# A quarter of the turned keys held in PSUM between the layers, and a norm's factor moved into the softmax, in a two-layer decode kernel

## The chip, the cores and the metric

The kernel runs on one core of a Trainium2 chip, in one launch. The metric is the device time of a whole execution in microseconds (us). Four executions of the kernel before gave a median of 1129.24 us, from 1121.21 to 1132.17.

## The reference, cut to what matters

Eight sequences (rows) decode one token each. Two blocks alternate, each twice: an attention block with a cache, and an MLP.

```python
B, Sq, D = 8, 1, 448
Hq, Hkv, Sk, Dh = 16, 8, 4096, 256          # F = 1792, all bfloat16

def _A_ref(x, k_cache, v_cache, wq, wo):     # x is normed
    q = (x @ wq)...                          # B, Hq, Sq, Dh
    scores = einsum("bhqd,bhkd->bhqk", q, k) * (Dh ** -0.5)
    p = softmax(scores); o = einsum("bhqk,bhkd->bhqd", p, v)
    return o... @ wo

x = A_x
x = x + _A_ref(_layernorm(x), A_k_cache, A_v_cache, A_wq, A_wo)
x = x + _B_ref(_layernorm(x), ...)           # norm, w3, gelu, w4
x = x + _A_ref(_layernorm(x), A_k_cache, A_v_cache, A_wq, A_wo)
x = x + _B_ref(_layernorm(x), ...)
```

Both attention blocks read the same caches. With a single token the shifts in the MLP's first half read only padding, so the kernel computes its second half alone. One row's keys of one KV head are 4096 x 256 bfloat16, 2 MiB (2048 KB in the profile), and its values as much. All keys and values are 256 MiB, and whatever is not kept in SBUF from the first layer is read again in the second.

## The kernel before, in words

**Tiles.** A key or value tile (row b, head h) lies on 128 partitions, 32 positions of 256 numbers on each, and is cut into four *quarters* of 4 KB a partition, 0.52 MB in all. SBUF has 30 slots of a quarter (`QUARTERS`, L14). `load` (L602) records one load for each quarter, the planner joins up to four neighbours into one DMA, and `issue_kv` (L590) writes it; L596 is the DMA itself, always on SyncE's queue (SP).

**A front** (L914) is the first half of one row's head in one layer: keys to softmax weights. Keys must be turned, because the scores contract over Dh. `transpose_piece` (L1091) turns half a quarter on TensorE into one of three PSUM banks `psT` (L1099), and DVE or ACT copies the bank back over the same slot (L1107, L1108). Then `sc` (L939) multiplies the turned quarter with the query into the bank `psS` (16 matmuls, L947), DVE copies the scores out and takes the maximum (L959, L962), GpSimd reduces it over partitions (L964), DVE scales and negates it into `nb` (L966), ACT takes two exponentials with `scale=1/16` and a bias from `nb` (L972), GpSimd sums (L976). **A back** (L982) loads the values, multiplies weights and values (32 matmuls `pv`, L1002), folds four partial rows into one (L1014, L1016, L1024, L1030) and multiplies with `wo` (L1049; for the last head of a row L900 and L903).

**What is kept.** In layer 1 (`layer == 0` in the code) heads 3 to 7 are the kept heads (`KEEP_K = 5`): their turned keys stay in SBUF, so that layer 2 of the same row need not load and turn them. Head 7 also keeps its four value quarters (`KEEP_V = 4`). That is 24 of 30 slots by the end of a row's layer 1; six slots are left as a ring through which everything else passes, until the scores of layer 2 free the kept keys again. Heads 0 to 2 are the free heads.

**The border between the layers.** For each row b: fronts and backs of its kept heads, head 7 last; then `mid` (L1131): the MLP (`mlp` L839), which gives x2, then `sums` (L695) and `moments` (L712) for the second attention's norm, then the second layer's queries (`second_queries`, L1140) for head 7 here and for the other heads a little ahead of their fronts. Beside it run the backs of the next row's free heads (12 quarters of values, whose fronts were done before). Then the fronts and backs of layer 2, head 7 first (`l2_heads` counts down, `MIX` L27), and the next row's kept heads. `sums` gets sum and sum of squares of x2 from TensorE, `moments` makes mean, variance and 1/sqrt from them in ten small DVE instructions and a table `t_q` (mean times column sums of wq times 1/sqrt), and the query is `psM * rsy + t_q` (L1145): it waits for all of them.

**The order** is made before the launch by `Plan.schedule` (L131): it has a cost for every instruction, starts on each engine the ready one of the lowest priority number, and chooses for each load a slot and the wait on the matmul that used this slot last (`next_kv` L177). The programs of the engines are then fixed. SP is in order: a load that waits for its slot holds all later loads. Where TensorE would be idle, `filler` (L1266) puts matmuls that compute nothing into a free `psT` bank (L1268)[...].

Of the kernel before, what the change touches and what calls it, by code (L numbers as in the profile page):

```python
# [6 lines left out]
P = 128  # L7
B = 8
D = 448
# [10 lines left out]
RSQRT_STEPS = ((0.703952253, 1.681914091), (0.5, 1.5000003))  # L20
KEEP_K = 5
KEEP_V = 4
MARGIN4, MARGIN2 = 6, 2
REP = 24
AT = (-4, -3, -2)
# [418 lines left out]
def bass_interleave_layers__gqa_block_cached__mixer_s_mlp__decode_kernel(  # L444
# [58 lines left out]
    mom = sb("mom", [P, 3, B], f32)  # L503
    cs_q = sb("cs_q", [P, 32], f32)
    cs_h = sb("cs_h", [P, 14], f32)
    t_q = sb("t_q", [P, 32], f32)
    t_h = sb("t_h", [P, 28], f32)
    var = sb("var", [P, 2, B], f32)
    rsi = sb("rsi", [P, 2, B], i32)
# [185 lines left out]
    def sums(src, skey, n):  # L695


        def mm(t):
            for r in range(n):
                for kc in range(4):  # L700
                    last = t.matmul(psM[:, SC + r * (n + 2):SC + (r + 1) * (n + 2)],
                                    wide(src[:, kc, r:r + 1]), src[:, kc, 0:n + 2],
                                    start=(kc == 0), stop=(kc == 3))
            return last
        pe(mm, 4 * n, rd=[skey, "one"], wr=["psM"], banks=[M])
# [3 lines left out]
        i = r * (n + 2) + n + 1  # L709
        return mom[:, i // B, i % B:i % B + 1]  # L710

    def moments(second, cs, cskey, t_, tkey, n):  # L712


        k = n * (n + 2)
        mo = mom[:, :, :].rearrange("p c n -> p (c n)")[:, 0:k]
        v0 = var[:, 0, 0:n]
        dv(lambda v: v.tensor_single_scalar(mo, psM[:, SC:SC + k], 1.0 / D, ALU.mult),
           rd=["psM"], wr=["mom"], banks=[M])
# [12 lines left out]
        rsqrt(c, n)  # L732
        w = cs.shape[1]
        for r in range(n):
            dv(lambda v, r=r: v.tensor_scalar(t_[:, r * w:(r + 1) * w], cs[:, :], minus_mean(n, r),
                                              rsy[:, c - 1, r:r + 1], ALU.mult, ALU.mult),
               rd=["mom", "rsy", cskey], wr=[tkey] if r == 0 else [(tkey, r)])

    def norm(src, skey, second, B):

# [98 lines left out]
    def mlp(src, skey, n, dst, dkeys):  # L839
# [6 lines left out]
        if few:  # L846

            sums(src, skey, n)
            moments(True, cs_h, "cs_h", t_h, "t_h", n)
# [61 lines left out]
    KEPT_V = {HKV - 1: range(4 - KEEP_V, 4)}  # L911
    done = {}

    def front(layer, b, h):  # L914
# [3 lines left out]
        fronts[0] += 1  # L918
        par, nr, nm = 0, free_p.pop(0), g % NS
        ps, bk = psS, "S"  # L920
        kept_k, kept_v = state.pop((0, b, h)) if layer else ({}, {})
        keep_k = KEPT_K.get(h, ()) if layer == 0 else ()
        if layer == 0:
            def rhs(c):
# [4 lines left out]
                return q2T[b % 2][:, 4 * h + 2 * c:4 * h + 2 * c + 2]  # L929
            qk = [("q2", b, h)]  # L930
        ks = dict(kept_k)
        fresh = [u for u in range(4) if u not in ks]
        ks.update(load(A_k_cache, b, h, fresh, keep_k))
        for u in range(4):
            if u in fresh:
                for pc in range(2):
                    transpose_piece(ks[u], pc)

            def sc(t, u=u, q=ks[u]):  # L939
                last = None  # L940
                for s in range(8):
                    i = 8 * u + s


                    for c in range(2):
                        a = slot_ap(q, s * 256, 256)
                        last = t.matmul(ps[:, 2 * i:2 * i + 2 * REP], a[:, c:256:2],  # L947
                                        bcast(rhs(c), REP, 1), start=(c == 0), stop=(c == 1))
# [17 lines left out]
        plan.op("dve", lambda v: v.tensor_single_scalar(nb[nm][:, :], gm[nm][:, :], -INV_SQRT_DH,  # L966
                                                        ALU.mult), 0.15, "max",
                rd=[("gm", nm)], wr=[("nb", nm)], prio=hi)

        for jj in range(2):  # L970
            def ex(a, jj=jj):
                return a.activation(pT[nr][:, :, :].rearrange("p i j -> p j i")[:, jj, :],  # L972
                                    sview[:, jj, :], ACT.Exp, bias=nb[nm][:, jj:jj + 1],
                                    scale=INV_SQRT_DH, accum_out=rs[nr][:, jj:jj + 1])
            plan.op("act", ex, 0.5, "exp", rd=[("nb", nm), ("sS", nm)], wr=[("pT", nr, jj), ("rs", nr, jj)], prio=hi)
# [4 lines left out]
        state[layer, b, h] = ({u: ks[u] for u in keep_k}, kept_v, nr)  # L980

    def back(layer, b, h):  # L982

        kept_k, vs, nr = state.pop((layer, b, h))
        free_p.append(nr)
        keep_v = KEPT_V.get(h, ()) if layer == 0 else ()
        g = backs[0]
# [96 lines left out]
               rd=["psM", ak], wr=[ok] + (["x3all" if b < B - 2 else "xf"] if layer else []), banks=[M],  # L1084
               name="acc", prio=hi)
        if layer == 0:
            state[layer, b, h] = (kept_k, {u: vs[u] for u in keep_v})

    tcount = [0]

    def transpose_piece(i, pc):  # L1091
        bank = tcount[0] % NT
        tcount[0] += 1

        def tr(t):
            last = None
            for s in range(4):
                src = slot_ap(i, (4 * pc + s) * 256, 256).bitcast(f32)
                last = t.transpose(psT[bank][:, s * P:(s + 1) * P], src, ident_f[:, :])  # L1099
# [4 lines left out]
        def ev(e):  # L1104
            dst = slot_ap(i, pc * 1024, 1024).bitcast(f32)
            if e is nc.vector:
                return e.tensor_copy(dst, psT[bank][:, :])  # L1107
            return e.copy(dst, psT[bank][:, :])  # L1108
        v = plan.op("ev", ev, {"dve": 0.71, "act": 0.6}, "ev", rd=[("psT", bank)],
                    wr=[("s", i, pc)], banks=[("T", bank)])  # L1110
        a.tbank = v.tbank = bank

    s_out = nc.alloc_semaphore("s_out")

# [25 lines left out]
    def second_queries(b, h, prio):  # L1140

        q, src = q2T[b % 2], x2c[b % 2]
        pe(lambda t: q_mms(t, range(4 * h, 4 * h + 4), lambda kc: src[:, kc, 0:1], psM, SC,
                           1, QW), 16, rd=[("x2", b)] + WQ, wr=["psM"], banks=[M], prio=prio)
        dv(lambda v: v.scalar_tensor_tensor(  # L1145
            q[:, 4 * h:4 * h + 4].rearrange("p (c j) -> p c j", c=2),
            psM[:, SC:SC + 4].rearrange("p (j c) -> p c j", c=2), rsy[:, 0, 0:1],
            t_q[:, 4 * h:4 * h + 4].rearrange("p (c j) -> p c j", c=2), ALU.mult, ALU.add),
           rd=["psM", "rsy", "t_q"], wr=[("q2", b, h)], banks=[M], prio=prio)


    dma_once("x", [(x_row[:, 0:D], A_x[:, 0, :], 7168), (x_row[:, D + P:], A_x[:, 0, 3 * P:D], 1024)],
# [174 lines left out]
```

## Time and profile before

| | us |
|---|---|
| median of four executions | 1129.24 |
| the profiled execution | 1130.02 |
| its span, first to last instruction | 1128.2 |
| TensorE busy, of the span | 967.5 (86%) |
| DVE busy | 552.9 (49%) |
| ACT busy | 280.9 (25%) |
| GpSimd busy | 97.6 (9%) |

The mean granted TensorE clock is 0.933. SP's queue moves 446.80 MB in 54784 packets. A page of the profile has the busy shares (part 1), forty slices of the span (part 2: busy tenths, granted clock, share of the 16 DMA engines, GB/s), the DMA queues (3), the chain that ended last (4), and groups of instructions by line with busy time, mean duration in ns and the idle time before them (5). Windows give the same for chosen stretches.

### The profile page before, as it was taken

The page shows a single profiled execution, that of the slowest core. Times are in us where ns is not written, and L with a number is a line of the kernel's source. Part 1 is how long each engine was busy: PE and PEld are TensorE (multiplying, and loading weights), DVE is VectorE, ACT ScalarE, POOL GpSimd, SP SyncE. Part 2 cuts the span into 40 slices and gives each one's busy share as a digit, 9 for nine tenths or more (in the row PEclk, how much of TensorE's full clock was granted, in tenths as well). Part 3 has the DMA queues.
Part 4 walks back from the last instruction along what each step waited for, and adds up shares of the span by engine and source line. Part 5 has one row for each costly group of instructions (what it writes and reads, how often), then busy time and mean ns, then how long its engine had stood idle before and what let it go on. Part 6 is the DMA issues. An engine that isn't in the chain of part 4 may idle for free.

```text
span 1128.2 us, 42331 instructions
## 1 busy us (share of the span) xinstructions
PE 967.5 (86%) x19458; PEld 775.0 (69%) x19458; DVE 552.9 (49%) x1745; ACT 280.9 (25%) x848; POOL 97.6 (9%) x275
## 2 busy tenths in 40 slices
PE   5888888898889897898889887989878998798897
PEld 4677566775669756686567765778566885686674
DVE  4345435455355544555346553565535654365444
ACT  1133112341124301243023410234112330142030
POOL 0001010010100100010010000110010010110010
PEclk9899999999889979899899988999999998999899
DMA  9999999999999999999999999999999999999993
GB/s 329 409 425 421 384 404 424 424 423 380 413 423 425 419 334 418 424 424 417 360 425 424 423 386 384 423 424 422 383 413 424 423 400 378 424 421 405 358 361 154
DMA packets 54962, 449.50 MB, mean 398 GB/s; under 512 B 5872, under 2 KB 9088, under 8 KB 28032
## 3 DMA queue, kind: packets, MB, share of 16 engines
q1 hardware_dynamic: 54784, 446.80, 97.1%
q8 instruction: 152, 2.49, 0.9%
q14 instruction: 26, 0.21, 0.0%
HBM read 446.77 MB, written 0.01 MB: 396 GB/s over the span
## 4 chain that ended last, share of the span: by engine, by line
PE 53%; DMA 36%; issue 5%; DVE 4%; SPq 1%; POOL 0%; ACT 0%
DMA kv<-in_A_k_cache_dram 21%; PE psT L1099 21%; PE psS L947 14%; DMA kv<-in_A_v_cache_dram 14%; PE psP L1002 7%; PE psR L1049 3%; PE psT L1268 2%; PE psM L797 2%; DMA w3x_sb<-in_B_w_dram 1%; PE psM L813 1%; DVE oS L1016 1%; DVE oS L1014 1%; PE psP L1024 1%; PE psM L900 1%; PE psM L903 1%
## 5 line engine op out<-in xcount | busy, mean ns | idle before, releaser
L1099 PE MATMUL psT<-ident_f,kv 128*128 128x128 f32 x2816 | 397.1, 287 | 18.3 <-DMA kv<-in_A_k_cache_dram 15.2
L1107 DVE COPY kv<-psT 128x512 f32<-128x512 f32 x379 | 261.4, 691 | 202.0 <-PE psT L1099 201.1
L1099 PEld LDWEIGHTS psT<-ident_f,kv 128*128 128x128 f32 x2816 | 319.7, 146 | 36.2 <-DMA kv<-in_A_k_cache_dram 20.2
L1108 ACT COPY kv<-psT 128x512 f32<-128x512 f32 x325 | 190.2, 587 | 404.3 <-PE psT L1099 404.2
L1002 PE MATMUL psP<-kv,pT 128*2 128x256 bf16 x4096 | 175.4, 285 | 25.8 <-DMA kv<-in_A_v_cache_dram 18.6
L947 PE MATMUL psS<-q2T,kv 128*128 128x48 bf16 x4096 | 142.3, 187 | 27.5 <-issue 27.4
L947 PEld LDWEIGHTS psS<-q2T,kv 128*128 128x128 bf16 x4096 | 126.2, 99 | 56.7 <-issue 52.9
L972 ACT ACTIVATE pT<-sS,nb 128x32 bf16<-128x32 f32 x256 | 81.9, 327 | 332.3 <-DVE nb L966 332.2
L947 PEld LDWEIGHTS psS<-q1T,kv 128*128 128x128 bf16 x4096 | 137.4, 97 | 13.5 <-issue 8.9
L947 PE MATMUL psS<-q1T,kv 128*128 128x48 bf16 x4096 | 145.0, 184 | 1.3 <-issue 1.1
L1002 PEld LDWEIGHTS psP<-kv,pT 128*2 128x2 bf16 x4096 | 80.4, 83 | 66.7 <-DMA kv<-in_A_v_cache_dram 26.1
L964 POOL PARTITION_ALL_REDUCE gm<-pm x128 | 45.4, 354 | 795.4 <-DVE pm L962 781.5
L959 DVE COPY sS<-psS 128x64 f32<-128x64 f32 x128 | 28.7, 224 | 128.1 <-PE psS L947 123.5
L1024 PE MATMUL psP<-sel,oS 128*128 128x2 bf16 x512 | 32.3, 166 | 51.6 <-DVE oS L1016 48.4
L1024 PEld LDWEIGHTS psP<-sel,oS 128*128 128x128 bf16 x512 | 24.2, 99 | 71.7 <-DVE oS L1016 66.4
L1049 PE MATMUL psR<-wo_sb,oT 128*1 128x448 bf16 x448 | 68.0, 388 | 6.1 <-DVE oT L1030 5.7
L1014 DVE CAST oS<-psP 128x256 bf16<-128x256 f32 x128 | 54.0, 422 | 36.8 <-PE psP L1002 33.9
L976 POOL PARTITION_ALL_REDUCE Db<-rs x128 | 51.0, 398 | 202.6 <-ACT pT L972 202.6
L1268 PE MATMUL psT<-ident_b 128*128 128x512 bf16 x169 | 58.3, 428 | 0.0
L1016 DVE TENSOR_TENSOR oS<-psP,oS 128x256 bf16<-128x256 f32 x128 | 54.2, 423 | 3.3
L972 ACT ACTIVATION_READ_ACCUMULATOR pT<-sS,nb 128x1 f32 x256 | 48.3, 189 | 0.0
L1030 DVE TENSOR_TENSOR oT<-psP,rc 128x4 bf16<-128x4 f32 x128 | 20.4, 159 | 46.0 <-PE psP L1024 42.0
(139 smaller groups left out, 519.4 us busy)
## 6 DMA issues: line engine op xcount, KB each, us to landing
kv<-in_A_k_cache_dram SPq DMA_DIRECT2D x78, 2048.0 KB, 21.9
kv<-in_A_v_cache_dram SPq DMA_DIRECT2D x57, 2048.0 KB, 19.8
kv<-in_A_v_cache_dram SPq DMA_DIRECT2D x130, 512.0 KB, 7.7
kv<-in_A_v_cache_dram SPq DMA_DIRECT2D x55, 1024.0 KB, 10.7
kv<-in_A_k_cache_dram SPq DMA_DIRECT2D x10, 1024.0 KB, 12.7
kv<-in_A_k_cache_dram SPq DMA_DIRECT2D x14, 512.0 KB, 8.3
kv<-in_A_v_cache_dram SPq DMA_DIRECT2D x4, 1536.0 KB, 13.9
wo_sb<-in_A_wo_dram SPq DMA_DIRECT2D x1, 3584.0 KB, 46.5
```

The source lines that it names most:

```text
L947: last = t.matmul(ps[:, 2 * i:2 * i + 2 * REP], a[:, c:256:2], bcast(rhs(c), REP, 1), start=(c == 0), stop=(c == 1))
L972: return a.activation(pT[nr][:, :, :].rearrange("p i j -> p j i")[:, jj, :], sview[:, jj, :], ACT.Exp, bias=nb[nm][:, jj:jj + 1], scale=IN ...
L976: plan.op("pool", lambda gp: gp.partition_all_reduce(Db[nr][:, :], rs[nr][:, :], P, RO.add), 0.5, "sum", rd=[("rs", nr, 0), ("rs", nr, 1)] ...
L1002: last = t.matmul(ps[g4:g4 + 2, PV0:PV0 + DH], pT[nr][:, i, :], slot_ap(q, s * 256, 256), start=(i < 4), stop=(i >= 28), skip_group_check= ...
L1014: plan.op("dve", lambda v: v.tensor_copy(oS[:, 0, :], po), 0.36, "o", rd=[("pv", par, x) for x in range(4)], wr=["oS0"], banks=[bk], prio=hi)
L1016: plan.op("dve", lambda v: v.tensor_tensor(oS[:, 1, :], po, oS[:, 0, :], ALU.subtract), 0.36, "o", rd=["oS0"] + [("pv", par, x) for x in r ...
L1024: last = t.matmul(ps[:, PV1 + 2 * c:PV1 + 2 * c + 2], oS[:, w, c:DH:2], sel[:, :], start=(w == 0), stop=(w == 1))
L1049: last = t.matmul(psR[r:r + 1, 0:D], oT[no][:, i % 2, i // 2:i // 2 + 1], wo_sb[:, a:a + D], start=(k == 1 and i < 2), stop=(k == HKV - 1 ...
L1099: last = t.transpose(psT[bank][:, s * P:(s + 1) * P], src, ident_f[:, :])
L1107: return e.tensor_copy(dst, psT[bank][:, :])
L1108: return e.copy(dst, psT[bank][:, :])
L1268: return t.matmul(psT[bank][:, :], ident_b[:, :], bcast(ident_b[:, :], 4, 1), start=True, stop=True)
```

## The change

1. **One quarter of head 7's keys is not kept in SBUF.** With `HOLD = 1`, head 7 keeps quarters 0 to 2. Quarter 3 is turned and copied to its slot as always, used for layer 1's scores, and its slot is given back. But its two `psT` banks are not used again: turned keys stay there until layer 2. There, after the scores of quarter 0, the two banks are copied (two more copies of L1107/L1108's kind) into quarter 0's slot, and quarter 3's scores read that slot. So 23 slots are kept at the border and seven are in the ring; head 7's front in layer 2 gives three slots back instead of four; between the layers one `psT` bank is left, for the filler.
2. **The second query's 1/sqrt moves.** The query becomes `cs_q * (-mean) + psM` and needs the mean alone. The factor 1/(16 sqrt(var)), `fac`, goes into `nb` and into the exponential's `scale`, now a per-partition operand, in layer 2. The query product (L797) no longer waits for the first DVE instruction of the norm, because the sums have columns of their own (`SC + 32`). `t_q` is gone.

In the programs that result, counted over the whole kernel: copies of turned keys 704 -> 720 (DVE 379 -> 398, ACT 325 -> 322), filler matmuls 169 -> 157, exponentials with the new scale operand 128 of 256, eight `t_q` gone and eight `fac` new. Loads by size (KB, keys and values together): 512: 144 -> 178; 1024: 65 -> 46; 1536: 6 -> 26; 2048: 135 -> 121.

```diff
+HOLD = 1
...
+    KEPT_K[HKV - 1] = range(4 - HOLD)
...
-        fresh = [u for u in range(4) if u not in ks]
+        fresh = [u for u in range(4) if u not in ks and u not in banks_of]
         ks.update(load(A_k_cache, b, h, fresh, keep_k))
+        hold = [u for u in range(4) if u not in keep_k] if keep_k else []
+        back_in = {}
+        for u in banks_of:
+            ks[u] = ks[u + HOLD - 4]
+            back_in[u + HOLD - 4] = u
...
-            if u not in keep_k:
+            if u in back_in:
+                for pc, bank in enumerate(banks_of[back_in[u]]):
+                    evacuate(ks[u], pc, bank).tbank = bank
+                    held_banks.remove(bank)
+            elif u not in keep_k:
                 o.frees = ks[u]
...
+        scale = fac[b % 2][:, 0:1] if layer else INV_SQRT_DH
+        plan.op("dve", lambda v: v.tensor_scalar(nb[nm][:, :], gm[nm][:, :], scale, -1.0, ALU.mult,
+                                                 ALU.mult), 0.15, "max", ...
-                                    scale=INV_SQRT_DH, accum_out=rs[nr][:, jj:jj + 1])
+                                    scale=scale, accum_out=rs[nr][:, jj:jj + 1])
...
-    def transpose_piece(i, pc):
+    def transpose_piece(i, pc, hold):
+        while tcount[0] % NT in held_banks:
+            tcount[0] += 1
         bank = tcount[0] % NT
...
-        sums(src, ("x2", b), 1)
-        moments(False, cs_q, "cs_q", t_q, "t_q", 1)
-        for h in heads:
+        sums(src, ("x2", b), 1, SC + 32)
+        second_queries(b, heads[0], None, lambda: dv(
+            lambda v: v.tensor_single_scalar(mom2[b % 2][:, :], psM[:, SC + 32:SC + 35], 1.0 / D, ALU.mult),
+            rd=["psM"], wr=[("mom2", b)], banks=[M]))
+        for h in heads[1:]:
             second_queries(b, h, None)
...
+        rsqrt(1, 1)
+        dv(lambda v: v.tensor_single_scalar(fac[b % 2][:, :], rsy[:, 0, 0:1], INV_SQRT_DH, ALU.mult),
+           rd=["rsy"], wr=[("fac", b)])
...
-            psM[:, SC:SC + 4]..., rsy[:, 0, 0:1],
-            t_q[:, 4 * h:4 * h + 4]..., ALU.mult, ALU.add),
+            cs_q[:, 4 * h:4 * h + 4]..., mom2[b % 2][:, 2:3],
+            psM[:, SC:SC + 4]..., ALU.mult, ALU.add),
```

More of the change, by code (lines that the diff above doesn't have):

```diff
@@ L505, in bass_interleave_layers__gqa_block_cached__mixer_s_mlp__decode_kernel @@
     cs_h = sb("cs_h", [P, 14], f32)
-    t_q = sb("t_q", [P, 32], f32)
+    mom2 = [sb(f"mom2{i}", [P, 3], f32) for i in range(2)]
+    fac = [sb(f"fac{i}", [P, 1], f32) for i in range(2)]
     t_h = sb("t_h", [P, 28], f32)
@@ L693, in second_var, with sums @@
                                      ALU.add), rd=["var"], wr=["var1"])
-    def sums(src, skey, n):
+    def sums(src, skey, n, at=SC):
         def mm(t):
@@ L700, in mm @@
                 for kc in range(4):
-                    last = t.matmul(psM[:, SC + r * (n + 2):SC + (r + 1) * (n + 2)],
+                    last = t.matmul(psM[:, at + r * (n + 2):at + (r + 1) * (n + 2)],
                                     wide(src[:, kc, r:r + 1]), src[:, kc, 0:n + 2],
@@ L710, in minus_mean, with moments @@
         return mom[:, i // B, i % B:i % B + 1]
-    def moments(second, cs, cskey, t_, tkey, n):
+    def moments(second, n):
         k = n * (n + 2)
@@ L732, in moments @@
         rsqrt(c, n)
[L733 to L737, printed above, removed]
     def norm(src, skey, second, B):
@@ L848, in mlp @@
             sums(src, skey, n)
-            moments(True, cs_h, "cs_h", t_h, "t_h", n)
+            moments(True, n)
+            for r in range(n):
+                dv(lambda v, r=r: v.tensor_scalar(t_h[:, r * 14:(r + 1) * 14], cs_h[:, :], minus_mean(n, r),
+                                                  rsy[:, 1, r:r + 1], ALU.mult, ALU.mult),
+                   rd=["mom", "rsy", "cs_h"], wr=["t_h"] if r == 0 else [("t_h", r)])
             pe(lambda t: h_mms(t, lambda kc: src[:, kc, 0:n], ch, 0, n, HW if n == 1 else 12), 56,
@@ L910, in bass_interleave_layers__gqa_block_cached__mixer_s_mlp__decode_kernel @@
     KEPT_K = {h: range(4) for h in range(HKV - KEEP_K, HKV)}
-    KEPT_V = {HKV - 1: range(4 - KEEP_V, 4)}
+    KEPT_K[HKV - 1] = range(4 - HOLD)
+    KEPT_V = {HKV - 1: range(max(4 - KEEP_V, 0), 4), HKV - 2: range(min(8 - KEEP_V, 4), 4)}
     done = {}
@@ L920, in front @@
         ps, bk = psS, "S"
-        kept_k, kept_v = state.pop((0, b, h)) if layer else ({}, {})
+        kept_k, kept_v, banks_of = state.pop((0, b, h)) if layer else ({}, {}, {})
         keep_k = KEPT_K.get(h, ()) if layer == 0 else ()
@@ L931, in front @@
         ks = dict(kept_k)
-        fresh = [u for u in range(4) if u not in ks]
+        fresh = [u for u in range(4) if u not in ks and u not in banks_of]
         ks.update(load(A_k_cache, b, h, fresh, keep_k))
+        hold = [u for u in range(4) if u not in keep_k] if keep_k else []
[3 more added lines that the diff above has]
+            back_in[u + HOLD - 4] = u
+        held = {}
         for u in range(4):
@@ L936, in front @@
                 for pc in range(2):
-                    transpose_piece(ks[u], pc)
+                    bank = transpose_piece(ks[u], pc, u in hold)
+                    if u in hold:
+                        held.setdefault(u, []).append(bank)
             def sc(t, u=u, q=ks[u]):
@@ L965, in front @@
                 0.46, "max", rd=[("pm", nm)], wr=[("gm", nm)], prio=hi)
-        plan.op("dve", lambda v: v.tensor_single_scalar(nb[nm][:, :], gm[nm][:, :], -INV_SQRT_DH,
-                                                        ALU.mult), 0.15, "max",
-                rd=[("gm", nm)], wr=[("nb", nm)], prio=hi)
+        scale = fac[b % 2][:, 0:1] if layer else INV_SQRT_DH
+        fk = [("fac", b)] if layer else []
+        plan.op("dve", lambda v: v.tensor_scalar(nb[nm][:, :], gm[nm][:, :], scale, -1.0, ALU.mult,
+                                                 ALU.mult), 0.15, "max",
+                rd=[("gm", nm)] + fk, wr=[("nb", nm)], prio=hi)
         for jj in range(2):
@@ L973, in ex @@
                                     sview[:, jj, :], ACT.Exp, bias=nb[nm][:, jj:jj + 1],
-                                    scale=INV_SQRT_DH, accum_out=rs[nr][:, jj:jj + 1])
-            plan.op("act", ex, 0.5, "exp", rd=[("nb", nm), ("sS", nm)], wr=[("pT", nr, jj), ("rs", nr, jj)], prio=hi)
+                                    scale=scale, accum_out=rs[nr][:, jj:jj + 1])
+            plan.op("act", ex, 0.5, "exp", rd=[("nb", nm), ("sS", nm)] + fk, wr=[("pT", nr, jj), ("rs", nr, jj)], prio=hi)
         plan.op("pool", lambda gp: gp.partition_all_reduce(Db[nr][:, :], rs[nr][:, :], P, RO.add),
@@ L979, in front @@
                 rd=[("Db", nr)], wr=[("rc", nr)], prio=hi)
-        state[layer, b, h] = ({u: ks[u] for u in keep_k}, kept_v, nr)
+        state[layer, b, h] = ({u: ks[u] for u in keep_k}, kept_v, held, nr)
     def back(layer, b, h):
-        kept_k, vs, nr = state.pop((layer, b, h))
+        kept_k, vs, held, nr = state.pop((layer, b, h))
         free_p.append(nr)
@@ L1086, in back, with evacuate, ev @@
         if layer == 0:
-            state[layer, b, h] = (kept_k, {u: vs[u] for u in keep_v})
+            state[layer, b, h] = (kept_k, {u: vs[u] for u in keep_v}, held)
     tcount = [0]
-    def transpose_piece(i, pc):
+    held_banks = set()
+    def evacuate(i, pc, bank):
+        def ev(e):
+            dst = slot_ap(i, pc * 1024, 1024).bitcast(f32)
+            if e is nc.vector:
+                return e.tensor_copy(dst, psT[bank][:, :])
+            return e.copy(dst, psT[bank][:, :])
+        return plan.op("ev", ev, {"dve": 0.71, "act": 0.6}, "ev", rd=[("psT", bank)],
+                       wr=[("s", i, pc)], banks=[("T", bank)])
+    def transpose_piece(i, pc, hold):
+        while tcount[0] % NT in held_banks:
+            tcount[0] += 1
         bank = tcount[0] % NT
@@ L1102, in transpose_piece @@
                 banks=[("T", bank)])
[L1104 to L1111, printed above, removed]
+        a.tbank = bank
+        v = evacuate(i, pc, bank)
+        if hold:
+            held_banks.add(bank)
+        else:
+            v.tbank = bank
+        return bank
     s_out = nc.alloc_semaphore("s_out")
@@ L1134, in mid, with second_queries @@
         mlp(x1c[b % 2], ("x1", b), 1, src[:, :, 0:1], [("x2", b)])
-        sums(src, ("x2", b), 1)
-        moments(False, cs_q, "cs_q", t_q, "t_q", 1)
-        for h in heads:
-            second_queries(b, h, None)
-    def second_queries(b, h, prio):
+        sums(src, ("x2", b), 1, SC + 32)
[3 more added lines that the diff above has]
+        for h in heads[1:]:
+            second_queries(b, h, None)
+        v0 = var[:, 0, 0:1]
+        m2 = mom2[b % 2]
+        dv(lambda v: v.scalar_tensor_tensor(v0, m2[:, 1:2], m2[:, 2:3], m2[:, 0:1], ALU.mult, ALU.add),
+           rd=[("mom2", b)], wr=["var"])
+        dv(lambda v: v.tensor_scalar(v0, v0, 0.0, LN_EPS, ALU.max, ALU.add), rd=["var"], wr=["var"])
+        rsqrt(1, 1)
+        dv(lambda v: v.tensor_single_scalar(fac[b % 2][:, :], rsy[:, 0, 0:1], INV_SQRT_DH, ALU.mult),
+           rd=["rsy"], wr=[("fac", b)])
+    def second_queries(b, h, prio, then=lambda: None):
         q, src = q2T[b % 2], x2c[b % 2]
@@ L1144, in second_queries @@
                            1, QW), 16, rd=[("x2", b)] + WQ, wr=["psM"], banks=[M], prio=prio)
+        then()
         dv(lambda v: v.scalar_tensor_tensor(
             q[:, 4 * h:4 * h + 4].rearrange("p (c j) -> p c j", c=2),
-            psM[:, SC:SC + 4].rearrange("p (j c) -> p c j", c=2), rsy[:, 0, 0:1],
-            t_q[:, 4 * h:4 * h + 4].rearrange("p (c j) -> p c j", c=2), ALU.mult, ALU.add),
-           rd=["psM", "rsy", "t_q"], wr=[("q2", b, h)], banks=[M], prio=prio)
+            cs_q[:, 4 * h:4 * h + 4].rearrange("p (c j) -> p c j", c=2), mom2[b % 2][:, 2:3],
+            psM[:, SC:SC + 4].rearrange("p (j c) -> p c j", c=2), ALU.mult, ALU.add),
+           rd=["psM", ("mom2", b), "cs_q"], wr=[("q2", b, h)], banks=[M], prio=prio)
     dma_once("x", [(x_row[:, 0:D], A_x[:, 0, :], 7168), (x_row[:, D + P:], A_x[:, 0, 3 * P:D], 1024)],
```

## The prediction

> **What bounds the kernel now.** I read the page first, then windows by stage, then what SP's queue waits for, then one border instruction by instruction. The page:
>
> ```profile
> span 1128.2 us, 42331 instructions
> ...
> GB/s 329 409 425 421 384 404 424 424 423 380 413 423 425 419 334 418 424 424 417 360 425 424 423 386 384 423 424 422 383 413 424 423 400 378 424 421 405 358 361 154
> ...
> PE 53%; DMA 36%; issue 5%; DVE 4%; SPq 1%; POOL 0%; ACT 0%
> ```
>
> The GB/s row has a flat top at 424 and about one dip for each row of the batch. The chain gives TensorE over half, yet wherever the row reads 424 a faster TensorE would find no data. So the question is what the dips cost. Columns of the windows: busy time and count by engine, granted TensorE clock, DMA share, GB/s.
>
> ```profile
> 292.00:396.00 104.00, 92.39 (x1737) 77.29 (x1737) 53.48 (x143) 33.46 (x97) 10.22 (x28) 0.93 1.01 423
> 396.00:428.00 32.00, 27.46 (x639) 18.44 (x641) 14.04 (x66) 1.66 (x9) 1.81 (x5) 0.79 0.92 341
> 1038.00:1058.00 20.00, 16.73 (x373) 10.01 (x372) 9.61 (x47) 0.21 (x1) 0.00 (x0) 0.83 0.91 330
> 1072.00:1084.00 12.00, 11.63 (x246) 10.19 (x244) 6.15 (x17) 4.86 (x14) 1.11 (x3) 0.96 0.86 282
> 1110.00:1128.20 18.20, 13.20 (x251) 8.36 (x248) 8.07 (x37) 0.23 (x1) 0.00 (x0) 0.89 0.03 13
> ```
>
> Between borders DMA is the bound (423 GB/s). A window's loss is its length times (1 - rate/424). For the eight borders, 120-152, 260-292, 396-428, 532-564, 664-696, 796-828, 920-964 and 1038-1058 us, with 383, 376, 341, 366, 358, 379, 376 and 330 GB/s, that is 3.1 + 3.6 + 6.3 + 4.4 + 5.0 + 3.4 + 5.0 + 4.4 = 35.2 us. 1072-1084 loses 4.0, the tail after the last load 17.6, the first 120 us 8.5. Only the 35.2 is in reach of this change: the tail is the last MLP, which keeps its code.
>
> What holds the loads at a border, 396 to 428 us:
>
> ```profile
> SPq L596 <- PE psP L1002: 13.2, 9, 2.9
> SPq L596 <- PE psP L1024: 6.9, 2, 6.1
> SPq L596 <- PE psS L947: 4.5, 2, 4.0
> ```
>
> L1002 is a value product, the last user of a slot: SP waits for slots. In the trace's landing times a half-megabyte load issued at 404.14 us, with little ahead of it, lands at 408.63: 4.5 us. Six slots at full rate (0.524 MB / 424 GB/s = 1.24 us each) go round in 7.4 us, so a quarter may stay 2.9 us between landing and release. TensorE exceeds that: the MLP's products run from 408.75 to 411.38, and values that had landed wait behind them. Two landings then come 2.0 and 1.65 us late (at 411.86 and 419.95).
>
> **The seventh slot.** It removes nothing from any engine; it lets 1.24 us more data be on its way at each pause: 4.1 us of stay instead of 2.9. Each border has at least one hole as long as a quarter when its small ones are added; those that lose most (third, fourth, fifth, eighth: 4.4 to 6.3 us) have two. Four borders x 2 and four x 1 quarters = 12 x 1.24 = **-14.9 us**. Bounds: 0, if TensorE's own pace is what SP waits for, and -28 (7/6 of the rate over the some 25 us of each border, with no border gaining more than it loses). I take 14.9 because the long waits are on releases whose data had already come. At 1072-1084 the kept keys are being released and no slot count is short: 0.
>
> **The shorter chain to the second queries.** From x2 to the first query, DVE at the same border:
>
> ```profile
> 411.48 0.17 DVE L892 SCALAR_TENSOR_TENSOR x2c<-psM,base 128x5 bf16<-128x5 f32 x1 [3.49 <-PE psM L903]
> ...
> 412.64 0.16 DVE L718 TENSOR_SCALAR mom<-psM 128x3 f32<-128x3 f32 x1 [0.19 <-PE psM L701]
> ...
> 415.25 0.30 DVE L735 TENSOR_SCALAR t_q<-cs_q,mom,rsy 128x32 f32<-128x32 f32 x1
> 415.59 0.22 DVE L1145 SCALAR_TENSOR_TENSOR q2T<-psM,rsy,t_q 128x4 bf16<-128x4 f32 x1
> ```
>
> Ten instructions stand between L718 and L1145, from 412.80 to 415.59. Afterwards sums and query product run back to back (the product takes 0.45 us, formerly from 413.27 because it waited for L718), then `mom2`, then the query at about 413.4-413.6: 2 us earlier. The norm's ten instructions still run, behind it, some 2 us on DVE, under head 7's four score groups (0.55 us each), the score copy (0.22), maximum (0.22) and GpSimd's 0.35; `fac` is there in time. With no such cover it costs the 2 us back. Head 7's slots come free 2 us earlier, but only holes after x2 gain, about the last of each border, and the new slot has filled most of it: 0.4 x 8 = **-3 us**, bounds 0 and -10 (half of 20 us still lost).
>
> **The held banks.** The turning and the copy in layer 1 stay; 16 copies are added, 0.69 us on DVE or 0.59 on ACT by their rows below, 10 us in all, on engines at 49% and 25%. New wait: quarter 3's scores in head 7's second front wait for both copies, which wait for quarter 0's scores. Behind that wait TensorE has a back's fold (L1024), query products, wo rows and head 6's scores; behind DVE's copy stand a back's two casts (0.42 each) and head 7's maximum. In the new program two value products (8 matmuls each, 0.5 us at the border) and two score groups (0.55 each) stand between: 2.1 us of cover. ACT is free. DVE's copy comes behind seven to eight instructions of the norm (0.2 each), so it ends 0.25 + 1.4 + 0.7 = 2.3 us after quarter 0's scores at worst. Exposed: 0 to 1 us; I take 0.15 x 8 = **+1 us**. Head 7 gives back three slots instead of four, which is the seventh slot paid back when it is no longer needed: 0.
>
> **More, smaller loads.** 21 more DMAs on SP (0.4 us each to issue, while SP waits most of the time), and 34 more of 0.5 MB. The Trainium skill, "DMA: Bandwidth & Descriptors", speaks against it: section "Anatomy of one DMA" gives a fixed 2.0 us for each (its fit is for the GpSimd path), and "Bandwidth" says to batch to 1 MiB or more. Paid in series, 21 x 2.0 = +42 us, and the change would lose. The trace shows loads queued behind one another: where others stand ahead, landings of 0.5 MB are 1.28 us apart (median), 1 MB 2.49, 1.5 MB 3.72 and 2 MB 4.91. So 34 x 1.28 - 19 x 2.49 + 20 x 3.72 - 14 x 4.91 = **+1.9 us**. I follow the trace; the fixed part is what makes a lone load take 4.5 us, and that is counted in the slot's round.
>
> **Exponentials with a pointer scale.**
>
> ```profile
> L1107 DVE COPY kv<-psT 128x512 f32<-128x512 f32 x379 | 261.4, 691 | 202.0 <-PE psT L1099 201.1
> L1108 ACT COPY kv<-psT 128x512 f32<-128x512 f32 x325 | 190.2, 587 | 404.3 <-PE psT L1099 404.2
> L972 ACT ACTIVATE pT<-sS,nb 128x32 bf16<-128x32 f32 x256 | 81.9, 327 | 332.3 <-DVE nb L966 332.2
> ```
>
> 128 of the 256 get `fac` as scale. No row here shows such a form. The skill's "ScalarE: Activation LUTs", section "What ACT_TABLE_LOAD costs", adds about 93 ns for each [128,1] pointer operand: 327 -> 420 ns, 12 us of ACT's time over the kernel (an estimate). Taken at the nearest row, where bias is already a pointer, the price is nothing. Between 0 and +12 I take nearly nothing: TensorE's waits for ACT's exponentials are 0.6 us in the whole trace, and a back stands a front behind. Only head 7's can show, 2 x 0.09 x 8 = +1.5; I put **+0.5**. `nb` takes a second operand on DVE with 2 columns: 0.
>
> **Sum.** 1130.0 - 14.9 - 3 + 1 + 1.9 + 0.5 = **1115.5**, against the profiled execution's own 1130.02, which is 0.8 over the median: 1115 us, 1.3% faster.
>
> **Rivals.** *A slot is worth once a border, and the chain nothing* (30%): after the first hole SP has caught up with TensorE, whose pace then rules: TensorE is busy 27.5 of 32 us at 396-428. Then 8 x 1.24 = -9.9, +3.4 for the costs: 1123.5, no change that can be measured. For it: busy TensorE there. Against: it waits for data even there (1.3 us for values from 392 to 412).
>
> *Both work fully* (15%): the rate at the borders rises by 7/6 and the last hole closes: -25 - 5 + 3 = 1103.
>
> *TensorE's clock falls at the borders, and the kernel is slower* (14%). The fillers use `psT` banks that are free; two of three are now held just where the clock is weakest (0.50 from 408 to 416 us, though TensorE's row is busy all the 8 us; 0.79 over the 32), and 12 of 169 fillers are gone. A border has 27 us of TensorE work at a clock near 0.87: each 0.05 less costs 27 x 0.05/0.87 = 1.55 us, or 12 in all. From 0.06 on the 14.5 gained are used up; at 0.12 less, +29 - 14.5 gives 1145. Against: one bank suffices for a filler at a time, and the new order has nine of them where the old has ten.
>
> *The change doesn't do what it says* (7%): SP is in order and each slot is fixed beforehand; if the seventh is assigned to a load stuck behind a later one, it lies idle. Only chain and costs remain: 1130.5.
>
> **How the numbers follow.** The main case has 34%; within it 1108 to 1122. A measurement of this kernel can tell about 1% (11 us) from no change. Faster by over 1% (below 1118): most of the main case (25), all of the full one (15), a quarter of the once-a-border one (8) = 0.48. Slower by over 1% (above 1140.5): most of the clock case = 0.11. The rest 0.41. The range leaves out the far ends of the full case and of the clock case: 1103 to 1134.
>
> **What would show it.** Right: border windows at 375 to 400 GB/s instead of 330 to 383, stages between unchanged at 423; SP's waits on L1002's counterpart shorter; first query some 2 us after x2 instead of 4; tail 17 to 18 us. Wrong: granted clock at borders under 0.8 on average (the clock); TensorE waiting for a copy of held keys in front of head 7's last score group by over 1 us; rates at borders unchanged while SP still waits for value products (TensorE's pace), or rates below 423 between borders (small loads).

## The result, and the profile after

The changed kernel takes 1122.51 us in the median (43 executions, 1118.24 to 1126.34) against 1127.31 us (64 executions) for the kernel before: a ratio of 0.9964, 95% interval 0.9953 to 0.9975 (the quotient of the two medians, 0.9957, lies inside it). The forecast was 1115 us and 1.3% faster. The direction is right and the size is not: 0.36% is less than a third of what was forecast, and below the 1% that I had called no change. The profiled execution took 1125.22 us, against 1130.02 us for the profiled one before.

The page of the kernel after:

```profile
span 1123.4 us, 42352 instructions
...
GB/s 335 407 425 420 385 390 425 423 419 387 406 424 426 417 348 417 425 422 420 380 422 425 424 399 399 423 424 420 385 413 424 426 387 371 397 423 414 369 398 158
...
PE 57%; DMA 30%; issue 6%; DVE 5%; ACT 1%; POOL 1%; SPq 0%; POOLq 0%
```

The flat top is where it was and the dips are all still there. Windows of the kernel after (busy time and count by engine, granted clock, DMA share, GB/s):

```profile
120.00:152.00 32.00, 24.98 (x600) 17.16 (x598) 11.93 (x61) 2.79 (x10) 1.11 (x3) 0.89 0.98 375
396.00:428.00 32.00, 27.10 (x615) 17.49 (x614) 13.51 (x65) 2.61 (x10) 1.52 (x5) 0.75 0.96 357
430.00:530.00 100.00, 87.41 (x1688) 74.45 (x1684) 54.76 (x143) 32.85 (x94) 9.83 (x27) 0.97 1.01 423
530.00:562.00 32.00, 26.52 (x632) 18.99 (x634) 14.00 (x66) 2.62 (x10) 1.85 (x5) 0.85 0.98 384
664.00:696.00 32.00, 27.17 (x657) 18.42 (x657) 14.55 (x68) 2.61 (x10) 2.07 (x6) 0.84 1.00 390
1038.00:1058.00 20.00, 16.98 (x431) 11.31 (x430) 12.23 (x57) 0.80 (x2) 0.12 (x1) 1.00 0.98 372
1072.00:1084.00 12.00, 9.80 (x224) 8.25 (x220) 5.56 (x16) 4.00 (x13) 1.51 (x4) 1.00 1.00 401
1106.00:1123.40 17.40, 14.47 (x271) 8.73 (x265) 8.48 (x39) 0.23 (x1) 0.00 (x0) 0.87 0.02 8
```

Between borders 423 GB/s, and a tail of 17.4 us: both as forecast. On the windows of the forecast the eight borders now read 375, 378, 357, 385, 390, 381, 374 and 372 GB/s, where they read 383, 376, 341, 366, 358, 379, 376 and 330 before: four clearly more, the others as before or less, and the third still below the 375 to 400 that I had expected. The window from 1072 to 1084 us, from which I had expected nothing, went from 282 to 401 GB/s. What SP waits for at the third border, from 390 to 430 us, before and after:

```profile
SPq L596 <- PE psP L1002: 22.9, 12, 8.0
...
SPq L599 <- PE psP L1021: 22.6, 10, 5.8
SPq L599 <- PE psS L960: 6.6, 5, 4.1
```

L1021 is the value product (formerly L1002): with seven slots, too, SP waits for slots of values, and as long as before. I had expected these waits to be shorter. They are not a measure of the loss, since SP also waits for slots in stretches that run at 423 GB/s.

The shorter way to the query is there. DVE and TensorE at the same border:

```profile
412.41 0.17 DVE L894 SCALAR_TENSOR_TENSOR x2c<-psM,base 128x5 bf16<-128x5 f32 x1 [4.10 <-PE psM L905]
...
414.18 0.15 DVE L1167 TENSOR_SCALAR mom<-psM 128x3 f32<-128x3 f32 x1
414.37 0.22 DVE L1187 SCALAR_TENSOR_TENSOR q2T<-cs_q,mom,psM 128x4 bf16<-128x4 f32 x1
```

```profile
413.90 1.02 PE L1021 MATMUL psP<-kv,pT 128*2 128x256 bf16 x16
414.86 0.27 PE L1043 MATMUL psP<-sel,oS 128*128 128x2 bf16 x4
415.41 0.67 PE L960 MATMUL psS<-q2T,kv 128*128 128x48 bf16 x16
416.00 0.35 PE L1068 MATMUL psR<-wo_sb,oT 128*1 128x448 bf16 x2
416.02 0.38 PE L1021 MATMUL psP<-kv,pT 128*2 128x256 bf16 x4
```

The query is ready 2.0 us after x2 instead of 4.1. But x2 itself comes at 412.41 instead of 411.48, and the first score group (L960) waits in TensorE's queue behind two value products and a fold. Means over the eight borders, from the trace (us; x1 is the MLP's input and hT the input of its second product; a step runs from the end of one instruction to the end, or for the first scores the start, of the next):

| | x1 to hT | x2 to first query | query to first scores | x1 to end of head 7's scores |
|---|---|---|---|---|
| before | 5.02 | 4.13 | 1.32 | 16.94 |
| after | 5.46 | 1.59 | 2.25 | 15.76 |

Of 2.5 us saved between x2 and the query, 1.2 are left at the end of head 7's scores: 0.9 go in the wait between query and scores, and 0.4 between x1 and hT.

### The profile page after: what moved, and what is told of

Read it like the earlier page. It is cut to its first block, busy times and chain, and to the rows that moved or that the text cites. A ratio compares the mean times of both kernels' runs of the same rounds, so it can differ in the third digit from the quotient of the medians.

```text
span 1123.4 us, 42352 instructions
## 1 busy us (share of the span) xinstructions
PE 962.2 (86%) x19446; PEld 772.9 (69%) x19446; DVE 563.1 (50%) x1764; ACT 290.9 (26%) x845; POOL 97.6 (9%) x275
## 4 chain that ended last, share of the span: by engine, by line
PE 57%; DMA 30%; issue 6%; DVE 5%; ACT 1%; POOL 1%; SPq 0%; POOLq 0%
DMA kv<-in_A_k_cache_dram 22%; PE psT L1131 20%; PE psS L960 15%; PE psP L1021 9%; DMA kv<-in_A_v_cache_dram 8%; PE psR L1068 3%; PE psM L794 2%; PE psT L1310 2%; PE psM L902 1%; PE psP L1043 1%; DVE oS L1035 1%; DVE oS L1033 1%; PE psM L905 1%; PE psM L810 1%; ACT pT L991 1%
## 5 line engine op out<-in xcount | busy, mean ns | idle before, releaser
L1115 DVE COPY kv<-psT 128x512 f32<-128x512 f32 x398 | 274.0, 691 | 197.5 <-PE psT L1131 195.3
L1131 PEld LDWEIGHTS psT<-ident_f,kv 128*128 128x128 f32 x2816 | 316.1, 145 | 53.3 <-DMA kv<-in_A_k_cache_dram 34.9
L1021 PE MATMUL psP<-kv,pT 128*2 128x256 bf16 x4096 | 178.5, 292 | 15.1 <-DMA kv<-in_A_v_cache_dram 8.3
L960 PE MATMUL psS<-q2T,kv 128*128 128x48 bf16 x4096 | 141.6, 186 | 27.6 <-issue 27.2
L960 PEld LDWEIGHTS psS<-q2T,kv 128*128 128x128 bf16 x4096 | 126.2, 99 | 54.1 <-issue 49.6
L960 PEld LDWEIGHTS psS<-q1T,kv 128*128 128x128 bf16 x4096 | 135.5, 97 | 17.0 <-issue 12.3
L960 PE MATMUL psS<-q1T,kv 128*128 128x48 bf16 x4096 | 145.1, 184 | 2.2 <-issue 2.1
L1021 PEld LDWEIGHTS psP<-kv,pT 128*2 128x2 bf16 x4096 | 85.1, 85 | 53.4 <-issue 16.6
L991 ACT ACTIVATE pT<-sS,nb,fac 128x32 bf16<-128x32 f32 x128 | 52.7, 418 | 182.0 <-DVE nb L985 182.0
L991 ACT ACTIVATE pT<-sS,nb 128x32 bf16<-128x32 f32 x128 | 40.9, 326 | 81.9 <-DVE nb L985 81.9
L1310 PE MATMUL psT<-ident_b 128*128 128x512 bf16 x157 | 52.0, 420 | 0.0
L794 PE MATMUL psM<-x2c,wq_sb 128*128 128x24 bf16 x768 | 36.7, 184 | 6.0 <-issue 5.9
## 6 DMA issues: line engine op xcount, KB each, us to landing
kv<-in_A_v_cache_dram SPq DMA_DIRECT2D x56, 2048.0 KB, 17.6
kv<-in_A_k_cache_dram SPq DMA_DIRECT2D x32, 512.0 KB, 12.2
```

What stands on the lines that cost most here:

```text
L794: last = t.matmul(bank[:, at + i * step:at + i * step + copies], w, r, start=(kc == 0), stop=(kc == 3))
L1021: last = t.matmul(ps[g4:g4 + 2, PV0:PV0 + DH], pT[nr][:, i, :], slot_ap(q, s * 256, 256), start=(i < 4), stop=(i >= 28), skip_group_check= ...
L1310: return t.matmul(psT[bank][:, :], ident_b[:, :], bcast(ident_b[:, :], 4, 1), start=True, stop=True)
```

## The experiments

Two measures serve all of them. The ratio to before, from executions on the same chip, decides. For the reason I use *holes*: landings of loads follow one another in the trace, and whatever a landing is later than its size explains (1.275, 2.50, 3.72 and 4.91 us for 0.5 to 2 MB behind other loads), over 0.2 us, is a hole. Holes in front of 0.5 and 1 MB loads lie for the most part at the borders, and those in front of larger ones in the streams between. There is one profile of each program, so holes show directions more than sizes, and a profiled execution can be faster or slower than the median of its program.

**One part at a time.** The query's new form alone, `q_only` (edit against the kernel after):

```diff
-HOLD = 1
+HOLD = 0
```

> The second query's new form alone: all four key quarters of head 7 stay in SBUF as before, six ring slots, nothing held in PSUM. Theory 'pace' (at a border TensorE's queue, which stands in one order, sets when slots are given back, and what helped is the shorter way to the query): 0.996 to 0.998 of before, so nearly all of the 0.9964. Theory 'slot' (what helped is the seventh slot): 0.999 to 1.001.

1.0025 (1.0006 to 1.0044). In its trace the mean way from x2 to the query is 1.49 us, yet from query to scores it is 3.14: TensorE's order put more in between.

The slot alone, `hold_only`, is the change without its second part (the old `mid`, `second_queries` and scale; one line of the edit against the kernel after):

```diff
-        scale = fac[b % 2][:, 0:1] if layer else INV_SQRT_DH
+        scale = INV_SQRT_DH
```

> The held quarter and the seventh slot alone, with the old queries (1/sqrt and t_q in the query, immediate scale in the exponentials). Theory 'pace': 0.999 to 1.002, the slot pays for no more than the smaller loads and the 16 copies. Theory 'slot': 0.995 to 0.997. The prediction's sum for this part alone was -14.9 + 1 + 1.9 = -12 us, 0.989.

0.9951 (0.9932 to 0.9970). "Pace", my first theory after the result, falls in both runs, as far as one order of the program can tell.

**Slots without PSUM.** Room for more comes from reading `wo` in place of `w4`.

```diff
-    w4_sb = sb("w4_sb", [P, 14 * D], bf)
+    w4_sb = wo_sb
...
-QUARTERS = 30
+QUARTERS = 31        # or 33
```

> The kernel before with w4 not loaded and not stored: the MLP reads wo's place instead (so its second product uses other numbers), which leaves room in SBUF. Still 30 slots, six in the ring. It is the base for more slots. Both theories: w4's 1.6 MB at 424 GB/s is 3.8 us less, 0.996 to 0.998.

0.9956 (0.9935 to 0.9977): the 3.8 us of the load that is left out lie inside this interval.

> As s30 (w4 neither loaded nor stored, wo read in its place), with 33 slots: nine in the ring, nothing held in PSUM, old queries. Theory 'slot': three more slots are worth at least twice what one is, 8 to 20 us under s30 (0.978 to 0.990 of before). Theory 'pace': within 3 us of s30 (0.993 to 0.999).

0.9868 (0.9848 to 0.9887), 11.3 us under s30, some 3 us either way: three slots, 3.8 us each. Holes at the borders in the two traces: 33.5 and 10.3 us. The trace of s30 is of its slowest execution (1127.64 us, 6.2 over its median), so this pair shows too large a fall.

> As s30 (w4 neither loaded nor stored, wo read in its place), with 31 slots: seven in the ring, nothing held in PSUM. Theory 'each slot is worth about half a quarter's time at each border' (hold_only was 5.3 us under before, s33 11.3 us under s30): 4 to 6 us under s30, 0.990 to 0.992 of before. If holding in PSUM costs something, s31 is lower than that; the prediction's 14.9 us for the slot would be 0.983.

0.9950 (0.9930 to 0.9970): 0.06% under s30, with an interval of some 0.3% on that difference, so the 4 to 6 us that I had expected lie just outside. By this run a seventh slot is worth between nothing and some 4 us in this order, and not 14.9. Its border holes are 19.7 us, so far fewer than in s30's trace, but those in the streams are 17.6 instead of 11.3.

**The way to the query, pulled and pushed.** `early_q` makes the second queries before the MLP, from x1 instead of x2:

```diff
-        mlp(x1c[b % 2], ("x1", b), 1, src[:, :, 0:1], [("x2", b)])
-        sums(src, ("x2", b), 1)
+        sums(x1c[b % 2], ("x1", b), 1)
         moments(False, cs_q, "cs_q", t_q, "t_q", 1)
         for h in heads:
             second_queries(b, h, None)
+        mlp(x1c[b % 2], ("x1", b), 1, src[:, :, 0:1], [("x2", b)])
```

> The kernel before with the second layer's queries made from x1 instead of x2, ahead of the MLP (other numbers in the second layer's queries; the MLP still runs and its x2 is still added at the end). The queries are ready some 10 us earlier at each border, with six ring slots. Theory 'loads do not wait for the query' (the query's way is covered by ring loads that do not need it): 0.994 to 1.003. Theory 'the way counts, and q_only had an unlucky order': 0.985 or less, as head 7's slots come free long before the ring has run dry.

0.9967 (0.9945 to 0.9988). In its trace the query is ready 4.2 us after x1 instead of 12.2, so 8 us earlier, and head 7's scores end 3.5 us earlier. That brings 3.7 us over eight borders, no more than another order can. `late_q` goes the other way:

```diff
-        for half, three in RSQRT_STEPS:
+        for half, three in RSQRT_STEPS + RSQRT_STEPS[1:] * extra:   # extra = 5 for the second queries
```

> The kernel before with five more Newton steps for the second queries' 1/sqrt: 15 more DVE instructions of about 0.2 us between x2 and the first query at each border, 3 us. Theory 'loads do not wait for the query': 0.998 to 1.006, since the slots of values are given back meanwhile. Theory 'the way counts': 8 x 3 = 24 us, 1.015 to 1.022.

1.0093 (1.0058 to 1.0128): 10.5 us, between the two theories. In its trace the way from x2 to the query is 8.5 us instead of 4.1, so 4.4 us longer at each border and not the 3 I had counted, and head 7's scores end 2.6 us later (19.5 us after x1 instead of 16.9). Of 35 us added to the query, three tenths show in the time. The way to the query is just covered: longer costs three tenths of what is added, shorter brings no more than another order does.

**What a new order alone does.** All these edits also change the planner's order and its slots. `order106` changes nothing else, only the factor by which the planner takes loads to be faster than nominal:

```diff
-    FASTER = 1.05
+    FASTER = 1.06
```

> The kernel before with one number of its planner changed (it takes loads to be 1.06 instead of 1.05 times the nominal rate): same work, another order of instructions and another choice of slots. It measures what a new order alone does. Theory 'differences of 0.3% are an order's luck': anything from 0.996 to 1.004, so that q_only's 1.0025 says no more than that nothing was gained. Otherwise 0.999 to 1.001.

0.9964 (0.9943 to 0.9985), the very ratio of the change. So one comparison in one order can't tell a part's worth. I took the kernel before, each part and the whole change in three orders.

> The kernel before with the planner's number at 1.04: another order of the same work. Theory 'a new order is worth up to 0.4% either way': 0.996 to 1.004.

0.9984 (0.9963 to 1.0005).

> The whole change with the planner's number at 1.06, to be read against order106 (0.9964), not against before. Theory 'the change itself is worth some 0.4% in any order': 0.991 to 0.994. Theory 'a new order explains it': 0.994 to 1.000, within 0.3% of order106 on either side.

0.9937 (0.9918 to 0.9956), 0.27% under order106.

> The whole change with the planner's number at 1.04, to be read against order104. Theory 'the change itself': 0.3 to 0.5% under order104. Theory 'a new order explains it': within 0.3% of order104 on either side, and with the pairs at 1.05 and 1.06 a mean gain under 0.2%.

0.9948 (0.9927 to 0.9969), 0.36% under order104.

> The held quarter and seventh slot alone (old queries) with the planner's number at 1.06, to be read against order106 (0.9964). Theory 'the slot is worth 0.5% by itself': 0.990 to 0.993. Theory 'a new order explains it': 0.994 to 0.999.

0.9969 (0.9949 to 0.9989), 0.05% over order106: read alone, this run would have said that the slot is worth nothing.

> The held quarter and seventh slot alone, planner's number 1.04, against order104 (0.9984). Theory 'the slot carries the gain' (about 0.3% in the mean of three orders; so far -0.49% at 1.05 and +0.05% at 1.06): 0.994 to 0.997. Theory 'neither part alone is worth it, only both': 0.998 to 1.001.

0.9934 (0.9909 to 0.9958), 0.50% under order104.

> The second query's new form alone, planner's number 1.04, against order104 (0.9984). Theory 'the query form is worth nothing': mean over three orders (1.04, 1.05, 1.06) of its difference to the same order of before within 0.15% of zero; here 0.997 to 1.001. Theory 'it carries part of the gain': 0.995 to 0.997.

0.9957 (0.9935 to 0.9979), 0.27% under order104.

> The second query's new form alone, planner's number 1.06, against order106 (0.9964). 'Worth nothing': 0.994 to 0.998. 'Carries part of the gain': 0.991 to 0.994.

0.9968 (0.9951 to 0.9986), 0.04% over order106.

| planner's number | before | query form alone | slot alone | both |
|---|---|---|---|---|
| 1.04 | 0.9984 | 0.9957 | 0.9934 | 0.9948 |
| 1.05 | 1 | 1.0025 | 0.9951 | 0.9964 |
| 1.06 | 0.9964 | 0.9968 | 0.9969 | 0.9937 |
| mean | 0.9983 | 0.9983 | 0.9951 | 0.9950 |
| border holes, mean of three profiles | 25.9 us | 23.5 us | 17.6 us | 19.9 us |

The three runs of one column differ by 0.3 to 0.7%. In the means the slot is worth -0.32% or 3.6 us, the query form 0.00%, both -0.33%. Repeated executions leave about 0.16% each way on these differences, but orders scatter more. The table has six pairs with and without the slot, three without the query form and three with it: from -0.61% to +0.05%, in the mean -0.33%, and by their scatter some 0.27% each way. The six pairs for the query form run from -0.32% to +0.25%, in the mean 0.0%, some 0.25% each way. So the slot carries the gain, and its size is known only roughly.

With the slot alone the holes shrink by 8.3 us, and some 40 more half-megabyte loads (185 in the mean instead of 146) at 0.05 us each take 2 us back. That fits the profiled executions, whose spans are 6.2 us shorter in the mean (1117.7 instead of 1123.9); the 3.6 us come from all executions. Of the 8.3 us, 7.2 lie at the eight borders and the rest after 1068 us. The four borders to which I had given two holes (third, fourth, fifth, eighth) lose 1.5 us of holes each, the other four 0.3 each; with both parts of the change it is 1.1 and 0.15.

**What limits a border otherwise.** `early33` has nine slots and early queries, `short_mlp` leaves out most of the MLP's matmuls at the borders, `short33` has that and nine slots.

> Nine ring slots (w4 neither loaded nor stored, wo read in its place) and the second queries from x1 (other numbers), both at once. The borders lose some 35 us to missing slots or to the way to the query; each limit alone gave -0.9% (s33 against s30) and -0.3% (early_q). Theory 'two limits of almost equal length': together clearly more than their sum, 0.960 to 0.975. Theory 'they add': 0.982 to 0.986. Theory 'a third limit, TensorE's own pace': no better than s33, 0.985 to 0.989.

0.9852 (0.9824 to 0.9880), 0.16% under s33 and inside its interval. There are not two equal limits that only give way together.

```diff
-            for kc in range(4):
+            for kc in kcs:               # range(1) for one row, else range(4)
...
-                for fc in range(14):
+                for fc in fcs:           # range(1) for one row, else range(14)
```

> The kernel before with most of the single-row MLP's matmuls left out at each border (14 of 56 in its first product, 5 of 70 in its second; other numbers): some 107 matmuls and 3 us less on TensorE between x1 and x2, in six of which the values' products stood still. early_q has shown that an earlier query alone brings 0.3%. Theory 'TensorE's own pace at the border': well beyond that, 8 x 2 to 8 x 3 us, 0.979 to 0.988. Theory 'six slots are the limit whatever TensorE does': 0.994 to 0.999.

0.9934 (0.9908 to 0.9960): 7.4 us, 0.9 a border of the 3 that are taken from TensorE. It lies between the two theories, and its interval reaches into the second. The run moves the query, too: it is ready 1.9 us earlier after x1, and head 7's scores end 3.2 us earlier, so it does not part TensorE's work from the way to the query.

> As short_mlp, with nine ring slots (w4 neither loaded nor stored, wo read in its place). s33 was 0.9868 and early33 0.9852. Theory 'TensorE's own pace is the limit that is left with nine slots': 0.970 to 0.980. Theory 'what is left is the loads themselves (their size, instruction fetches), no engine': 0.984 to 0.988.

0.9826 (0.9802 to 0.9850), 0.42% under s33, again between them and with an interval that reaches the second. Border holes are down to 7.5 us, but holes in the streams of large loads are 20.9 (14.6 before; s33 has 19.6 already). So more slots bring most, less work on TensorE with an earlier query brings some more, and neither ends the losses. What makes the holes in the streams was not tried, and stays open.

## Why the prediction was wrong, point by point

**The seventh slot** (-14.9 us) is the step that failed: the sum "four borders x 2 and four x 1 quarters", each at its full 1.24 us. The direction was right: one more slot makes the holes at the borders smaller, and three more bring 11.3 us (s33). The size was not: the holes at the eight borders shrink by 7.2 us instead of 14.9, and the time by 3.6 us in the mean of three orders (6.2 us in the profiled executions, from which the holes are read), after costs of some 2 us.

Three things are wrong in the working. First, the 35.2 us in reach, and 4.0 at 1072-1084, were taken from a rate against 424 GB/s; by landings the same stretches have 30.9 us of holes in the execution I read, mostly because 0.5 MB loads take 1.275 us a quarter even with others ahead of them, and 25.9 in the mean of three orders. Second, small holes were added until they made a quarter, and a quarter was credited for them: those four borders got back 0.3 us each, by the mean of three profiles. Third, where a border had two holes the sum shortened both in full, as if the spare quarter were there anew for the second: those four got back 1.5 us each instead of 2.48. That the lead is used up at the first hole is my reading of it, and no run shows it by itself. The 0 for 1072-1084 was wrong the other way: holes after 1068 us shrink by 1.2 us.

The rival "a slot is worth once a border, and the chain nothing" had given 1123.5 us, 1 us from the 1122.51 measured, and I gave it 30%. Part of that nearness is luck. It starts, as my sum does, from a profiled execution that is 2.7 us above the median of before (1127.31), and it forecasts 6.5 us where 0.36% is 4.1. Its reason, that after the first hole SP has caught up with TensorE, is not shown either.

**The shorter way to the query** (-3 us) came out at 0.0%, by the scatter of the six pairs with 0.25% or 2.8 us either way, so probably less than forecast. At the query 2.5 us are real (4.13 to 1.59 us), and 0.9 of them go in the wait for TensorE behind it. (Between L718 and L1145 stood eleven instructions, t_q among them, and not ten.) early_q shows that 8 us would bring little more. My reading is that loads for values go on meanwhile; no run shows that by itself. The case to ask about was the other one: late_q shows that the cover is nearly used up.

**Held banks** (+1 us). TensorE's waits for turned keys' copies, in front of scores, are small in the whole trace after:

```profile
PEld psS L960 <- DVE kv L1115: 1.4, 4, 0.4
...
PEld psS L960 <- ACT kv L1116: 1.1, 3, 0.4
```

The longest is 0.4 us (before, such waits were 2.3 + 0.2 us). The cover of two value products and two score groups held, and the wait of over 1 us that would have spoken against the change is not there. What holding costs by itself no run separates.

**Smaller loads** (+1.9 us). In the trace after, landings of 0.5 MB behind others are 1.274 us apart, of 2 MB 4.90: the price was right, and the +42 us that loads paid in series would have cost are not there.

**Exponentials with a pointer scale** (+0.5 us). ACT in the kernel after:

```profile
L991 ACT ACTIVATE pT<-sS,nb,fac 128x32 bf16<-128x32 f32 x128 | 52.7, 418 | 182.0 <-DVE nb L985 182.0
...
L991 ACT ACTIVATE pT<-sS,nb 128x32 bf16<-128x32 f32 x128 | 40.9, 326 | 81.9 <-DVE nb L985 81.9
```

418 against 326 ns: 92 ns for another pointer operand, where the Trainium skill ("ScalarE: Activation LUTs", section "What ACT_TABLE_LOAD costs") states about 93, and 12 us of ACT's time. TensorE waits 1.2 us in all for such a result (before 1.3 + 0.6). So the figure was right for the instruction, and that the time hardly feels it was right, too; half a microsecond can't be measured here.

**The clock rival** (slower). The granted clock over the whole is 0.934 against 0.933, with 157 fillers for 169. Over 32 us around each of the eight borders its mean is 0.883 after and 0.875 before; in the three orders (1.05, 1.04, 1.06) it is 0.883, 0.905 and 0.920 against 0.875, 0.934 and 0.858. It varies from one profile to the next and does not fall consistently with the held banks. The rival took it that fillers hold the clock up; no run here leaves them out, so that is not shown.

**What the forecast left out** is that an edit which makes the planner write a new order moves the time by itself (0.36% in one other order of before; 0.16% in the second, which is not clear of no change). Forecast and result of a change of this size can be right or wrong by that alone; here it did not turn the sign, since the change gained 0.27 to 0.36% in each of three orders.

## What to carry to other kernels

Where a ring of buffers runs dry, count the missing time by landings against the spacing of loads of the same size, and in more than one execution. Credit one more slot with at most one load's time per dry stretch, not once for each hole in it, and with next to nothing where the holes are only small ones. A chain that is already covered by other work pays little when it is shortened, and a push in the other direction (add the same time, see what it costs) tells how near its edge it is. When a planner rewrites the order after each edit, measure the edit in several orders before you believe a few tenths of a per cent; the slot alone in another order (0.9934) and the whole change in another (0.9937) are both faster than the change as it stands.

## What the runs showed of the hardware that I had not expected

Landings keep a spacing that depends on load size even in a full queue: 1.274 us for 0.5 MB, 2.50 for 1 MB, 3.71 for 1.5 MB and 4.90 for 2 MB, so 4% less rate for the smallest. The same work with another static order on the engines ran at 0.9964 of its time (0.9943 to 0.9985).
